# Queries spread one unit later, key weights ahead of mish, and a quarter of the first wq block brought by GpSimd's queue

## The chip, the cores and the metric

The kernel runs on one core of a Trainium2 chip. The time is device microseconds of one execution, and what is compared is the median of several runs. Everything is float32.

## The reference

A decode step for 8 batches (one token each, D = 512), as a parallel block: attention over a cache and an MLP stand beside each other and both are added to x. There are 32 query heads and 8 key heads (4 queries to a key head), 8192 cached positions and a head size of 128.

```python
xn = _layernorm(x, axis=-1)
# attention: q from xn, keys and values from the cache
q = (xn @ wq).reshape(B, 1, 32, 128).transpose(0, 2, 1, 3)
scores = einsum("bhqd,bhkd->bhqk", q, repeat(k_cache, 4)) * 128 ** -0.5
o = einsum("bhqk,bhkd->bhqd", softmax(scores), repeat(v_cache, 4))
attn = o.transpose(0, 2, 1, 3).reshape(B, 1, 32 * 128) @ wo
# MLP: Dense -> Mish -> Dense, F = 1792
h = einsum("bsd,df->bsf", xn, w1) + b1
mlp = einsum("bsf,fd->bsd", h * tanh(softplus(h)), w2)
return x + attn + mlp
```

## The kernel before

The cache is the work: keys and values are 537 MB of the 561 MB that are read. They come in units. A unit is one batch and one pair of key heads (8 query heads); there are 4 pairs times 8 batches, so 32 units, numbered j = 8 * pair + batch. Each unit has 8.39 MB of keys and 8.39 MB of values, laid by the host so that each of the 128 partitions reads one contiguous row of 64 KB (`load_unit`).

All of it goes through one wide tile `kv` of 2.5 unit rows for each partition. `V_AT` is the place of values, the first row. `K_AT` gives two places for keys that overlap by half a row: keys of even units lie in the second row, keys of odd units half a row further. So the keys of unit j+1 may be loaded as soon as the first half of the scores of unit j is through, and the values of unit j as soon as the values of unit j-1 were used. Unit 0 is an exception: its keys lie in the values' place. The weights of the MLP (`w1_t`), the bias (`b1_sb`), x and the scratch of `mish` borrow the second row at the start; the loads of wo and w2 use `kv` at the end.

Nothing is reordered by a scheduler: the order in which the code is written is the order of each engine's queue, and waits come from the data. Nearly all loads are issued by SyncE (SP), in one queue, in order: the first pair's block of wq (`load_q(0)`, 2.10 MB into tile `ws`), the keys of unit 0, w1, the keys of unit 1, and then, for unit after unit, keys j+1 and values j. ScalarE's queue issues x and b1. GpSimd issues no load; it makes `ident`, `ones`, `perm` and clears `pt8`.

The start, before the first unit: GpSimd makes the identity; VectorE builds selection matrices from it (`perm`, `mask`, `bsel` and others, lines 146 to 166) and then does the layer norm (lines 170 to 183); TensorE turns the normalised x into `xn4` (for wq) and `xnT` (for w1); `selections` fills tile `tr` with a selection matrix; `project` multiplies `xn4` with `ws` into PSUM tile H, in two halves of 512 columns (L218), and turns the result into `qT`; `spread` multiplies 16 slices of `tr` with `qT` into PSUM tile X (L244) and copies them to `qr` (L251); `key_weights(0)` multiplies `qr` with `mask` on VectorE (L262) into `wk`, the stationary operand of the scores.

One unit in the loop (lines 441 to 471), in the order of the code: half of `scores(j)` on TensorE (L279), the issue of keys j+1, the other half, `softmax(j)` (a chain of small steps, from L291 to L312), `values(j-1)` on TensorE (L341), the issue of values j, `key_weights(j+1)` on VectorE, `turn(j)` (TensorE permutes the exponentials into X at L318, VectorE transposes X into `tr` at L323 and sums into `pt8` at L329), and `merge(j-1)`. In unit 0 `mish` stands in the place of `values`, ahead of the issue of values 0 and of `key_weights(1)`.

Every pair of key heads needs its own queries. With `LOAD_Q, MAKE_Q, SPREAD_Q = 4, 5, 6` the next block of wq is loaded at the end of batch 4 of a pair, `project` runs in batch 5 ahead of `turn`, and `selections` and `spread` run at the end of batch 6, after `turn` and `merge`. `selections` overwrites `tr`, which `turn` has just used.

Of the kernel before, what the change touches and what calls it, by code (L numbers as in the profile page):

```python
# [8 lines left out]
F32 = mybir.dt.float32  # L9
# [4 lines left out]
P = 128  # L14
B = 8
# [3 lines left out]
DH = 128  # L19
# [5 lines left out]
G = 4  # L25
NH = 2
TG = SK // (NH * G) // P
BW = 1024
CC = D // P
FG = F // G  # L30
FT = 4
FP = FG // FT
Q = P // G
# [4 lines left out]
ROW = NB * P * BW // P  # L38
# [13 lines left out]

V_AT = 0
K_AT = (ROW, ROW + ROW // 2)
W1_AT = ROW
# [1 line left out]
PLACES = 2 * ROW + ROW // 2  # L59


LOAD_Q, MAKE_Q, SPREAD_Q = 4, 5, 6


@with_exitstack
def kernel(
# [12 lines left out]
    nc = tc.nc  # L79
# [7 lines left out]
    kv = const.tile([P, PLACES], F32, name="kv")  # L87
# [13 lines left out]
    hsel = const.tile([P, H2], F32, name="hsel")  # L101
    isel = const.tile([P, TL], F32, name="isel")
    rsel = const.tile([P, H2], F32, name="rsel")
    gsel = const.tile([G, G, B], F32, name="gsel")
    xn4 = const.tile([P, CC, B], F32, name="xn4")
    xnT = const.tile([P, CC, B], F32, name="xnT")
    qr = const.tile([P, DI, H2 * B], F32, name="qr")
    xres = const.tile([P, P], F32, name="xres")
    oT = const.tile([P, NP, H2, B], F32, name="oT")
# [4 lines left out]
    def load_q(m):  # L114

        rows = wq.rearrange("j p f -> (j p f)").rearrange("(m p f) -> m p f", m=NP, p=P)
        nc.sync.dma_start(ws, rows[m])

    def load_unit(src, j, at):
        m, b = divmod(j, B)  # L120
        lo = (b * HKV + 2 * m) * NH * G
        t = kv[:, at : at + ROW]
        nc.sync.dma_start(
            t,
            src[lo : lo + NB].rearrange("j p f -> (j p f)").rearrange("(p f) -> p f", p=P),
        )
        return t
# [2 lines left out]
    low = kv[:B, W1_AT : W1_AT + 3 * D]  # L130
    x_sb, xc, sq = (low[:, i * D : (i + 1) * D] for i in range(3))
    nc.scalar.dma_start(x_sb, x)
    b1_sb = kv[:G, W1_AT + 7168 : W1_AT + 7168 + FG]
    nc.scalar.dma_start(b1_sb, b1.rearrange("(g f) -> g f", g=G))
    load_q(0)
    k_t = {0: load_unit(kT, 0, V_AT)}
    w1_t = kv[:, W1_AT : W1_AT + 7168].rearrange("p (j f) -> p j f", j=2 * CC)

# [19 lines left out]
    for d in range(2):  # L158
# [3 lines left out]
            axis=AX.XY,  # L162
        )
    nc.vector.tensor_copy(
        gsel, ident[:G, :G].rearrange("p (g o) -> p g o", o=1).to_broadcast([G, G, B])
    )


# [17 lines left out]
    for c in range(CC):  # L186
        nc.tensor.transpose(
            M[:, 32 + c * B : 32 + (c + 1) * B], xc[:, c * P : (c + 1) * P], ident[:B, :B]
        )
    nc.vector.tensor_copy(xn4.rearrange("p c b -> p (c b)"), M[:, 0:32])  # L190
    nc.vector.tensor_copy(xnT.rearrange("p c b -> p (c b)"), M[:, 32:64])
    for g in range(G):
# [17 lines left out]
    selections()  # L210


    def project():

        w = ws.rearrange("p (c f) -> p c f", c=CC)
        for d in range(2):
            for c in range(CC):
                nc.tensor.matmul(  # L218
                    H[Q * c : Q * c + B, :],
                    xn4[:, c, :],  # L220
                    w[:, c, d * 512 : (d + 1) * 512],
                    start=True,
                    stop=True,
                )
            qp = work.tile([P, 512], F32, name="e")
            nc.scalar.copy(qp, H)  # L226
            for h in range(REP):
                at = 192 + (d * REP + h) * B
                nc.tensor.matmul(  # L229
                    M[:, at : at + B],  # L230
                    qp[:, h * DH : (h + 1) * DH],
                    bsel[:, :B],
                    start=True,
                    stop=True,
                )
        qT = work.tile([P, H2 * B], F32, name="qT", bufs=1)
        nc.vector.tensor_scalar_mul(qT, M[:, 192 : 192 + H2 * B], DH**-0.5)
        return qT
# [18 lines left out]
    def key_weights(j):  # L257
        b = j % B
        w = WK[j] = work.tile([P, DI, 2, NH * G, REP], F32, name="wk", bufs=1)
        q = qr.rearrange("p i (d o h b) -> p i d o h b", d=2, o=1, b=B)[..., b]  # L260
        for d in range(2):
            nc.vector.tensor_mul(  # L262
                w[:, :, d],
                q[:, :, d].to_broadcast([P, DI, NH * G, REP]),
                mask[:, d * NH * G : (d + 1) * NH * G]
                .rearrange("p (o k r) -> p o k r", o=1, r=1)
                .to_broadcast([P, DI, NH * G, REP]),
            )
# [68 lines left out]
    def values(j, vt):  # L337
        for n in range(NJ):
            l, c = divmod(n, HALF)
            q = n % G  # L340
            nc.tensor.matmul(  # L341
                O[Q * q : Q * (q + 1), :],
                pt8[:, c, TL * l : TL * (l + 1), :].rearrange("p t h -> p (t h)"),
                vt[:, 512 * n : 512 * (n + 1)],
                start=(n < G),
                stop=(n >= NJ - G),
            )
        os = work.tile([P, DH], F32, name="os")
        nc.vector.tensor_scalar(os, O[:, :DH], isel[:, 0:1], None, op0=ALU.mult)  # L349
        for i in range(1, TL):  # L350
            nc.vector.scalar_tensor_tensor(  # L351
                os, O[:, DH * i : DH * (i + 1)], isel[:, i : i + 1], os, op0=ALU.mult, op1=ALU.add
            )
        return os
# [6 lines left out]

    def mish(w1_t, b1_sb, flat):
        hp = H[:, :FG]
        for g in range(G):
            nc.tensor.matmul(
                hp[Q * g : Q * g + B, :], gsel[:, g, :], b1_sb, start=True, stop=False
            )
        for c in range(CC):
            for g in range(G):
                nc.tensor.matmul(  # L370
                    hp[Q * g : Q * g + B, :],
                    xnT[:, c, :],
                    w1_t[:, c * 2 + g // 2, g % 2 * FG : (g % 2 + 1) * FG],
                    start=False,
                    stop=(c == CC - 1),
                )
        a, z, z2, one, h = (flat[:, FG * i : FG * (i + 1)] for i in range(5))
        nc.vector.tensor_copy(h, hp)
        nc.vector.scalar_tensor_tensor(a, h, -1.0, h, op0=ALU.mult, op1=ALU.max)
        nc.scalar.activation(z, a, AF.Exp, scale=-1.0)  # L380
        nc.vector.tensor_mul(z2, z, z)
        m = a
        nc.vector.tensor_single_scalar(m, h, 0.0, op=ALU.is_gt)
        nc.vector.tensor_scalar(one, z2, -1.0, 1.0, op0=ALU.mult, op1=ALU.add)
        nc.vector.tensor_mul(one, one, m)
        t1 = m
        nc.vector.tensor_add(t1, one, z2)
        t2 = z2
        nc.vector.tensor_scalar(one, one, -1.0, 1.0, op0=ALU.mult, op1=ALU.add)
        nc.vector.scalar_tensor_tensor(t2, z, 2.0, t1, op0=ALU.mult, op1=ALU.add)  # L390
        nc.vector.scalar_tensor_tensor(t1, one, 2.0, t2, op0=ALU.mult, op1=ALU.add)
        nc.vector.reciprocal(z, t1)
        nc.vector.tensor_mul(t1, t2, z)
        act = one
        half = FG // 2
        for e in range(2):
            nc.vector.tensor_mul(
                act.rearrange("p (i a e l) -> p e a l i", a=2, e=2, i=W2R)[:, e],
                h[:, half * e : half * (e + 1)].rearrange("p (a l i) -> p a l i", a=2, i=W2R),
                t1[:, half * e : half * (e + 1)].rearrange("p (a l i) -> p a l i", a=2, i=W2R),  # L400
            )
        turned = flat[:, 5 * FG : 6 * FG]
        nc.vector.transpose(turned, act)
        nc.vector.tensor_copy(aT, turned.rearrange("p (j q) -> p j q", q=Q)[:, :, :B])
# [27 lines left out]


    nc.sync.dma_start(w1_t, w1.rearrange("j p f -> p j f"))
    k_t[1] = load_unit(kT, 1, K_AT[1])
    qT = project()
    spread(qT)
    key_weights(0)

# [1 line left out]
    for j in range(UNITS):  # L441
        b = j % B
        more = j // B + 1 < NP

        k = k_t.pop(j)
        scores(j, k, j % 2 == 1, 0)
        if j == UNITS - 1:
            v_t[j] = load_unit(v, j, K_AT[0])
        elif j > 0:
            k_t[j + 1] = load_unit(kT, j + 1, K_AT[(j + 1) % 2])  # L450
        scores(j, k, j % 2 == 0, 1)
        WK.pop(j)
        lsel = softmax(j)
        os = None
        if j > 0:
            os = values(j - 1, v_t.pop(j - 1))
        else:
            mish(w1_t, b1_sb, kv[:, W1_AT : W1_AT + 6 * FG])
        if j + 1 < UNITS:
            v_t[j] = load_unit(v, j, V_AT)  # L460
            key_weights(j + 1)
        if more and b == LOAD_Q:
            load_q(j // B + 1)
        if more and b == MAKE_Q:
            qT = project()
        turn(j, lsel)
        if j > 0:
            merge(j - 1, os)
        if more and b == SPREAD_Q:
            selections()  # L470
            spread(qT)


    w_o = [kv[:, 4096 * m : 4096 * (m + 1)] for m in range(NP)]
# [28 lines left out]
        )  # L503
    for p, t in zip(parts[1:], w2_t[1:]):
        down(*p, t)
    res = work.tile([P, DH], F32, name="os")
    nc.vector.tensor_add(res, H[:, :P], xres)
    nc.sync.dma_start(out, res)

# [37 lines left out]
```

## Time and profile before

| | |
|---|---|
| median of 3 runs | 1332.83 us (1330.54 to 1333.72) |
| the profiled execution | 1329.46 us |
| its span in the profile | 1327.7 us |
| busy | PE 75%, PEld 26%, DVE 39%, ACT 3%, POOL 0% |
| mean granted TensorE clock | 0.869 |
| read from HBM | 561.01 MB, mean 423 GB/s over the span |

Times in the views are microseconds from the start of the span. PE is TensorE's matmul, PEld its weight load, DVE is VectorE, ACT ScalarE, POOL GpSimd, SP SyncE; a "q" behind an engine is its sequencer, which issues DMAs. A float32 matmul shows as two matmul instructions, so that the 32 matmuls of `scores` stand as x64. "DMA share" in a table of windows is the mean busy share of the 16 DMA engines; it can go a little over 1. The chain that ended last is the work followed back from the last instruction, each step to what released it.

### The profile page before, as it was taken

How to read it: one execution, taken by the hardware profiler on the slowest of the kernel's cores; microseconds unless marked ns; L12 is line 12 of the kernel's file. 1: busy time of each engine (PE TensorE's matmuls, PEld its weight loads, DVE VectorE, ACT ScalarE, POOL GpSimd, SP SyncE). 2: the span in 40 equal slices, each digit the busy share in tenths (PEclk: the TensorE clock that was granted, in tenths of full speed). 3: DMA queues.
4: the chain of work that ended last, by engine and by line, in shares of the span. 5: the costliest groups of instructions: out<-in, count | busy, mean ns of one | idle time of the engine just before them, and what ended most of it. 6: DMA issues, size and time to landing. Idle time of an engine off the chain costs nothing.

```text
span 1327.7 us, 11151 instructions
## 1 busy us (share of the span) xinstructions
PE 990.3 (75%) x5040; PEld 349.4 (26%) x5040; DVE 514.8 (39%) x728; ACT 40.2 (3%) x88; POOL 2.2 (0%) x9
## 2 busy tenths in 40 slices
PE   5688767878887678785877677788686687677666
PEld 3222222323222222233322222232332222222222
DVE  3464344431444433345243344413444423344421
ACT  1000000000000000000000000000000000000000
POOL 0000000000000000000000000000000000000000
PEclk9999888787988898877998788788697988888897
DMA  9999999998999999999999999999899999999998
GB/s 394 443 407 418 439 440 418 439 435 340 431 439 441 417 433 439 435 433 427 393 433 423 435 439 431 431 429 439 370 417 435 439 437 423 432 439 437 429 414 334
DMA packets 13591, 561.79 MB, mean 423 GB/s; under 512 B 1244, under 2 KB 1376, under 8 KB 4584
## 3 DMA queue, kind: packets, MB, share of 16 engines
q1 hardware_dynamic: 13520, 561.06, 98.2%
q8 instruction: 39, 0.64, 0.2%
q14 instruction: 8, 0.07, 0.0%
q10 hardware_dynamic: 24, 0.02, 0.0%
HBM read 561.01 MB, written 0.07 MB: 423 GB/s over the span
## 4 chain that ended last, share of the span: by engine, by line
DMA 65%; PE 29%; DVE 5%; ACT 1%; issue 0%; SPq 0%
DMA kv<-in_v 62%; PE o L341 19%; PE s L279 6%; DMA kv<-in_w 3%; PE x L244 2%; DVE pt L329 2%; PE x L318 1%; DVE tr L323 1%; DVE tr L205 0%; PE h L425 0%; DVE wk L262 0%; PE m L229 0%; PE h L218 0%; DVE nm L291 0%; PE h L370 0%
## 5 line engine op out<-in xcount | busy, mean ns | idle before, releaser
L279 PE MATMUL s<-kv,wk 128*64 128x512 f32 x2048 | 507.4, 659 | 165.7 <-DMA kv<-in_kT 153.1
L341 PE MATMUL o<-kv,pt 128*32 128x512 f32 x2048 | 258.5, 663 | 51.8 <-DMA kv<-in_v 42.2
L279 PEld LDWEIGHTS s<-kv,wk 128*64 128x64 f32 x2048 | 156.3, 152 | 491.6 <-issue 322.9
L329 DVE TENSOR_REDUCE pt<-tr 64x512 f32<-64x2048 f32 x64 | 241.4, 3771 | 1.6
L291 DVE TENSOR_REDUCE nm<-s 128x1 f32<-128x512 f32 x32 | 22.1, 692 | 413.5 <-PE s L279 413.5
L318 PE MATMUL x<-e,perm 128*128 128x512 f32 x256 | 126.7, 641 | 0.0
L341 PEld LDWEIGHTS o<-kv,pt 128*32 128x32 f32 x2048 | 68.2, 120 | 215.5 <-issue 161.2
L349 DVE TENSOR_SCALAR os<-o,isel 128x128 f32<-128x128 f32 x32 | 11.2, 351 | 261.1 <-PE o L341 261.1
L323 DVE STREAM_TRANSPOSE tr<-x 128x512 f32<-128x512 f32 x128 | 78.7, 673 | 0.0
L318 PEld LDWEIGHTS x<-e,perm 128*128 128x128 f32 x256 | 49.3, 203 | 75.1 <-issue 75.1
L262 DVE TENSOR_TENSOR wk<-qr,mask 128x512 f32<-128x512 f32 x64 | 62.9, 1023 | 8.7 <-ACT qr L251 8.7
L244 PE MATMUL x<-qT,tr 128*128 128x64 f32 x128 | 29.4, 424 | 37.7 <-DVE tr L205 34.7
L310 ACT ACTIVATE e<-s,nmx 128x512 f32<-128x512 f32 x32 | 22.0, 687 | 1058.0 <-DVE nmx L307 1058.0
L244 PEld LDWEIGHTS x<-qT,tr 128*128 128x128 f32 x128 | 27.9, 330 | 38.8 <-DVE tr L205 35.0
L351 DVE SCALAR_TENSOR_TENSOR os<-o,isel,os 128x128 f32<-128x128 f32 x96 | 33.7, 351 | 3.4
L292 PE MATMUL m<-ident,nm 128*1 128x128 f32 x32 | 8.6, 270 | 25.5 <-DVE nm L291 25.5
L303 PE MATMUL m<-ident,nx 1*128 1x1 f32 x32 | 7.0, 218 | 24.1 <-DVE nx L299 24.1
L358 PE MATMUL m<-hsel,os 128*128 128x8 f32 x64 | 12.4, 266 | 9.3 <-DVE rt L321 9.3
L312 DVE TENSOR_SCALAR lsel<-rsel,l 128x8 f32<-128x8 f32 x32 | 7.4, 231 | 30.4 <-ACT e L310 30.4
L321 DVE RECIPROCAL rt<-m 128x8 f32<-128x8 f32 x32 | 6.6, 207 | 29.7 <-PE m L319 29.7
L292 PEld LDWEIGHTS m<-ident,nm 128*1 128x1 f32 x32 | 2.5, 79 | 53.7 <-DVE nm L291 53.7
L229 PE MATMUL m<-bsel,e 128*128 128x8 f32 x64 | 11.8, 313 | 6.0 <-ACT e L226 6.0
(88 smaller groups left out, 165.7 us busy)
## 6 DMA issues: line engine op xcount, KB each, us to landing
ws<-in_wq SPq DMA_DIRECT2D x4, 2048.0 KB, 34.3
kv<-in_wo SPq DMA_DIRECT2D x4, 2048.0 KB, 24.3
kv<-in_w SPq DMA_DIRECT2D x1, 3584.0 KB, 26.6
kv<-in_w SPq DMA_DIRECT2D x1, 2048.0 KB, 35.6
kv<-in_w SPq DMA_DIRECT2D x1, 1024.0 KB, 20.7
kv<-in_kT SPq DMA_DIRECT2D x32, 29.6
kv<-in_v SPq DMA_DIRECT2D x32, 30.0
kv<-in_w SPq DMA_DIRECT2D x1, 512.0 KB, 20.5
```

The costliest lines, as they stand in the source:

```text
L229: nc.tensor.matmul(M[:, at : at + B], qp[:, h * DH : (h + 1) * DH], bsel[:, :B], start=True, stop=True,)
L244: nc.tensor.matmul(X[:, half, k * 64 : (k + 1) * 64], wide[:, half * 8 + k], qT, start=True, stop=True,)
L262: nc.vector.tensor_mul(w[:, :, d], q[:, :, d].to_broadcast([P, DI, NH * G, REP]), mask[:, d * NH * G : (d + 1) * NH * G] .rearrange("p (o ...
L279: nc.tensor.matmul(S[64 * c : 64 * (c + 1), :], w[:, i].rearrange("p d k h -> p (d k h)"), kk[:, i, c, :], start=(part == 0 and n == 0), s ...
L291: nc.vector.tensor_reduce(nm, S, axis=AX.X, op=ALU.max, negate=True)
L310: nc.scalar.activation(e, S, AF.Exp, bias=nmx, accum_out=l)
L318: nc.tensor.matmul(X[:, g], perm[:, g], e, start=True, stop=True)
L323: nc.vector.transpose(tr.rearrange("p (l t) c -> p t l c", t=TL)[:, tl], X.rearrange("p g (t q l) -> p t l g q", t=TL, q=PP)[:, tl],)
L329: nc.vector.tensor_reduce(pt8[half, :, :, d * REP : (d + 1) * REP].rearrange("p c y h -> p y c h"), tr[half].rearrange("p y (g c h) -> p y ...
L341: nc.tensor.matmul(O[Q * q : Q * (q + 1), :], pt8[:, c, TL * l : TL * (l + 1), :].rearrange("p t h -> p (t h)"), vt[:, 512 * n : 512 * (n ...
L351: nc.vector.scalar_tensor_tensor(os, O[:, DH * i : DH * (i + 1)], isel[:, i : i + 1], os, op0=ALU.mult, op1=ALU.add)
L358: nc.tensor.matmul(M[:, 168 : 168 + H2], os, hsel, start=True, stop=True)
```

## The change

- `SPREAD_Q` becomes 7. `spread` runs in batch 7, after `values` and the issue of the next load and ahead of `key_weights` of the next pair's first unit, and so ahead of `turn`. `selections` stays at the end of batch 6.
- In unit 0, `mish` comes after the issue of values 0 and after `key_weights(1)`. In it the bias is added after the products with w1, and by 8 matmuls of 224 columns for 4 of 448.
- The first block of wq is split. Three quarters (rows 0 to 383, 12 KB for each of 128 partitions) go to `ws` by SP as before. The last quarter (128 rows, 0.52 MB) goes to partitions 64 to 95 of `kv`, 16 KB for each, at the place where the keys of unit 1 will lie. GpSimd's queue brings it in four DMAs of eight partitions, each after one of four small DMAs for b1. These eight DMAs stand ahead of the making of the identity on GpSimd.
- For that, x is also turned into `xn3` (3 transposes) and `xnx` (4 matmuls to partitions 64 to 95), and `project(0)` has 7 terms for each half instead of 4. The keys of unit 1 are issued after `project(0)`, since they overwrite the quarter.
- The tile `os` has one buffer for two.

```diff
+D3 = 3
+XQ = slice(64, 96)
+XAT = ROW + ROW // 2
-LOAD_Q, MAKE_Q, SPREAD_Q = 4, 5, 6
+LOAD_Q, MAKE_Q, SPREAD_Q = 4, 5, 7
...
-    gsel = const.tile([G, G, B], F32, name="gsel")
+    gsel = const.tile([B, B, B], F32, name="gsel")
+    xn3 = const.tile([P, D3, B], F32, name="xn3")
+    xnx = const.tile([P, CC, B], F32, name="xnx")
...
-    b1_sb = kv[:G, W1_AT + 7168 : W1_AT + 7168 + FG]
-    nc.scalar.dma_start(b1_sb, b1.rearrange("(g f) -> g f", g=G))
-    load_q(0)
+    b1_sb = kv[:B, W1_AT + 7168 : W1_AT + 7168 + FG // 2]
+    q0 = wq[:CC].rearrange("j p f -> (j p) f")
+    q0_3 = ws[:, : D3 * BW]
+    q0_x = kv[XQ, XAT : XAT + CC * BW]
+    for r in range(4):
+        n = FG // 8
+        nc.gpsimd.dma_start(
+            b1_sb[:, n * r : n * (r + 1)], b1.rearrange("(g c f) -> c g f", g=B, c=4)[r]
+        )
+        nc.gpsimd.dma_start(
+            q0_x[r::4], q0[D3 * P :].rearrange("(e r i) f -> r e (i f)", r=4, i=CC)[r]
+        )
+    nc.sync.dma_start(q0_3, q0[: D3 * P].rearrange("(p i) f -> p (i f)", i=D3))
     k_t = {0: load_unit(kT, 0, V_AT)}
...
+    for c in range(D3):
+        nc.tensor.transpose(
+            M[:, 64 + c * B : 64 + (c + 1) * B], xc[:, c : D3 * P : D3], ident[:B, :B]
+        )
+    for c in range(CC):
+        nc.tensor.matmul(
+            M[XQ, 96 + c * B : 96 + (c + 1) * B],
+            xc[:, D3 * P + c :: CC],
+            ident[:B, :B],
+            start=True,
+            stop=True,
+        )
+    nc.vector.tensor_copy(xn3.rearrange("p c b -> p (c b)"), M[:, 64 : 64 + D3 * B])
+    nc.vector.tensor_copy(xnx[XQ].rearrange("p c b -> p (c b)"), M[XQ, 96:128])
...
-    def project():
+    def project(m):
         w = ws.rearrange("p (c f) -> p c f", c=CC)
+        terms = [(c, xn4[:, c, :], w[:, c]) for c in range(CC)]
+        if m == 0:
+            wx = q0_x.rearrange("p (c f) -> p c f", c=CC)
+            terms = [(c, xn3[:, c, :], w[:, c]) for c in range(D3)]
+            terms += [((c + D3) % CC, xnx[XQ, c, :], wx[:, c]) for c in range(CC)]
         for d in range(2):
-            for c in range(CC):
+            for n, (c, xt, wt) in enumerate(terms):
                 nc.tensor.matmul(
                     H[Q * c : Q * c + B, :],
-                    xn4[:, c, :],
-                    w[:, c, d * 512 : (d + 1) * 512],
-                    start=True,
-                    stop=True,
+                    xt,
+                    wt[:, d * 512 : (d + 1) * 512],
+                    start=(n < CC),
+                    stop=(n >= len(terms) - CC),
                 )
...
     nc.sync.dma_start(w1_t, w1.rearrange("j p f -> p j f"))
+    qT = project(0)
     k_t[1] = load_unit(kT, 1, K_AT[1])
-    qT = project()
     spread(qT)
     key_weights(0)
...
             os = values(j - 1, v_t.pop(j - 1))
-        else:
-            mish(w1_t, b1_sb, kv[:, W1_AT : W1_AT + 6 * FG])
         if j + 1 < UNITS:
             v_t[j] = load_unit(v, j, V_AT)
+            if more and b == SPREAD_Q:
+                spread(qT)
             key_weights(j + 1)
+        if j == 0:
+            mish(w1_t, b1_sb, kv[:, W1_AT : W1_AT + 6 * FG])
         if more and b == LOAD_Q:
             load_q(j // B + 1)
         if more and b == MAKE_Q:
-            qT = project()
+            qT = project(j // B + 1)
         turn(j, lsel)
         if j > 0:
             merge(j - 1, os)
-        if more and b == SPREAD_Q:
+        if more and b == SPREAD_Q - 1:
             selections()
-            spread(qT)
```

More of the change, by code (lines that the diff above doesn't have):

```diff
@@ L164 @@
     nc.vector.tensor_copy(
-        gsel, ident[:G, :G].rearrange("p (g o) -> p g o", o=1).to_broadcast([G, G, B])
+        gsel, ident[:B, :B].rearrange("p (g o) -> p g o", o=1).to_broadcast([B, B, B])
     )
@@ L347, in values @@
             )
-        os = work.tile([P, DH], F32, name="os")
+        os = work.tile([P, DH], F32, name="os", bufs=1)
         nc.vector.tensor_scalar(os, O[:, :DH], isel[:, 0:1], None, op0=ALU.mult)
@@ L363, in mish @@
         hp = H[:, :FG]
[L364 to L367, printed above, removed]
         for c in range(CC):
@@ L373, in mish @@
                     w1_t[:, c * 2 + g // 2, g % 2 * FG : (g % 2 + 1) * FG],
+                    start=(c == 0),
+                    stop=False,
+                )
+        for g in range(G):
+            for e in range(2):
+                nc.tensor.matmul(
+                    hp[Q * g : Q * g + B, e * (FG // 2) : (e + 1) * (FG // 2)],
+                    gsel[:, 2 * g + e, :],
+                    b1_sb,
                     start=False,
-                    stop=(c == CC - 1),
+                    stop=(e == 1),
                 )
@@ L505 @@
         down(*p, t)
-    res = work.tile([P, DH], F32, name="os")
+    res = work.tile([P, DH], F32, name="os", bufs=1)
     nc.vector.tensor_add(res, H[:, :P], xres)
```

## The prediction

> **What bounds the kernel now.** I read the page first, then the windows, then the chain of waits, then the timeline around each place that stood out. On the page, the digits of the DMA engines and the first line of the chain:
>
> ```profile
> DMA  9999999998999999999999999999899999999998
> ...
> q1 hardware_dynamic: 13520, 561.06, 98.2%
> ...
> DMA 65%; PE 29%; DVE 5%; ACT 1%; issue 0%; SPq 0%
> ```
>
> One queue, SP's, brings nearly all the bytes and keeps the 16 DMA engines busy. The transfers bound the kernel; a change pays only where the stream runs dry or would run dry. Windows show where (columns: stretch, its us, busy us of each engine, granted clock, DMA share, GB/s):
>
> ```profile
> 300.00:340.00 40.00, 34.70 (x172) 15.89 (x172) 7.97 (x16) 1.95 (x4) 0.00 (x0) 0.80 0.86 365
> 620.00:660.00 40.00, 33.83 (x174) 15.98 (x174) 9.21 (x19) 1.95 (x4) 0.00 (x0) 0.83 0.91 387
> 940.00:980.00 40.00, 33.55 (x172) 15.69 (x172) 9.09 (x18) 1.95 (x4) 0.00 (x0) 0.82 0.90 381
> 344.00:604.00 260.00, 198.92 (x986) 66.06 (x986) 100.25 (x137) 6.62 (x16) 0.00 (x0) 0.88 1.00 432
> ```
>
> Between pair boundaries the share is 1.00. At the three boundaries it is 0.86, 0.91 and 0.90, which is 0.33 x 40 = 13.2 us of lost streaming. The chain around the first boundary shows why, and its later rows how long the others take:
>
> ```profile
> 278.29 8.77 PE o L341 x64
> ...
> 301.22 1.80 DVE tr L205
> ...
> 303.07 3.69 PE x L244 x16
> ...
> 311.09 16.32 PE s L279 x64
> ...
> 363.05 8.81 PE o L341 x64
> ...
> 401.74 8.54 PE o L341 x64
> ...
> 600.34 7.07 PE o L341 x64
> ...
> 681.92 8.40 PE o L341 x64
> ...
> 919.27 8.77 PE o L341 x64
> ...
> 1002.85 10.06 PE o L341 x64
> ```
>
> An undisturbed unit takes 401.74 - 363.05 = 38.7 us, 19.35 for each of its two loads. Across a boundary two units take 84.8, 81.6 and 83.6 instead of 77.4: 7.4 + 4.2 + 6.2 = 17.7 us lost. In batch 6 TensorE stands between `turn` and L244 until VectorE has finished `turn` and `selections` (L205), then spreads until 311.0, and only then starts the scores of unit 7. The next keys wait for half of these scores:
>
> ```profile
> 287.12 0.33 SPq L123 DMA_DIRECT2D kv<-in_v  x1
> ...
> 320.56 0.33 SPq L123 DMA_DIRECT2D kv<-in_kT  x1
> ```
>
> The times from issue to landing of the two load lines, L123 (keys and values) and L117 (wq), in that order:
>
> ```profile
> DMA to landing us min/median/max: 21.8/29.8/45.6
> ```
>
> ```profile
> DMA to landing us min/median/max: 7.8/34.3/34.4
> ```
>
> The minimum, 21.8, is a load issued into a dry queue: 19.35 of transfer and 2.45 of latency. So a load must be issued 2.45 us before the one ahead of it has landed. Values 6, issued at 287.12, land about 29.8 later, at 316.9; keys 8 should have been issued by 314.5 and came at 320.56.
>
> **The change: spread behind the values.** Without spread in batch 6, scores 7 start when their keys land, 316.9 - 19.35 = 297.6, are half through at 297.6 + 8.2 = 305.8 (half of L279's 16.32), and keys 8 are issued there, 8.7 us early. The same work then stands in batch 7, and I look for what is late next. Values 6 land at 316.9 and take 8.8, to 325.7; values 7 are issued there, before spread, so SP's queue loses nothing. Spread takes 303.07 to 311.0, 8.0 us, to 333.7, and no longer waits for `selections`, which VectorE made a unit earlier. Then ScalarE's copy (0.6, by the gaps in the chain) and VectorE's key weights (1.9, L262 below), to 336.3, while TensorE does `turn` (about 4) to 338. Keys 8 landed at 336.3; scores 8 start at 338, and keys 9 are issued at 346.2. They are needed by 336.3 + 19.35 - 2.45 = 353.2. Seven us of cover remain, so no new gap. If that cover were gone, spread's 8 us would return as a gap one unit later.
>
> What comes back is between the lost share, 13.2, and the lost time of the units, 17.7. The second holds delays of single DMA engines (a load lands with its slowest engine), part of which may come back at other places. I take the middle, **15.5 us**.
>
> **Key weights ahead of mish.** The rows of the start that the rest needs:
>
> ```profile
> 0.73 0.59 ACTq L132 DMA_DIRECT2D kv<-in_x  x1
> ...
> 1.35 0.26 ACTq L134 DMA_DIRECT2D kv<-in_b  x1
> ...
> 1.38 0.53 POOL L142 MEMSET perm<- 128x512 f32 x1
> ...
> 2.40 0.64 DVE L151 COPY perm<-ident 128x16 f32<-128x16 f32 x8
> ...
> 9.96 0.57 PE L187 MATMUL m<-ident,kv 8*128 8x8 f32 x4
> ...
> 10.68 0.18 DVE L191 COPY xnT<-m 128x32 f32<-128x32 f32 x1
> ...
> 11.46 1.90 PE L218 MATMUL h<-ws,xn 128*8 128x512 f32 x8
> ...
> 12.07 8.05 SPq L123 DMA_DIRECT2D kv<-in_kT  x1
> ...
> 47.63 0.33 SPq L123 DMA_DIRECT2D kv<-in_v  x1
> ...
> 49.56 0.93 PE L365 MATMUL h<-kv,gsel 4*8 4x448 f32 x8
> ...
> 53.68 0.62 DVE L378 COPY kv<-h 128x448 f32<-128x448 f32 x1 [1.44 <-PE h L370]
> ...
> 65.15 0.22 DVE L404 COPY aT<-kv 128x112 f32<-128x112 f32 x1
> ...
> 65.28 1.92 DVE L262 TENSOR_TENSOR wk<-qr,mask 128x512 f32<-128x512 f32 x2
> ...
> 75.80 0.33 SPq L123 DMA_DIRECT2D kv<-in_kT  x1
> ```
>
> Keys 1, issued at 12.07 into a full queue (the 45.6 of the landings), land at 57.7; values 0 at 57.7 + 19.35 = 77.0. Keys 2 come at 75.80, 1.25 us after the 74.55 that would have kept the stream whole. Scores 1 had waited for L262, which stood behind mish. Ahead of mish it falls mostly into VectorE's 1.44 us of idling, mish ends at about 66 (half a us later), and scores 1 start when TensorE has done `turn`, at about 58. Keys 2, which overwrite mish's scratch too, are then issued at 66. Gain **1.2 us**. The bias matmuls (0.93 for four) become eight of half the width: at most 0.9 us more, under the cover of the 8 us by which keys 2 are now early. `os` with one buffer is free: its reader `merge` ends a unit before the next write.
>
> **The start.** Values 0 must be issued by 57.7 - 2.45 = 55.2, and they came at 47.63: a start later by up to 7.6 us costs nothing, and what is beyond is lost in full (keys 2 move along, since mish and scores 1 move as much as values 0). Two clocks can make it late.
>
> First GpSimd. It now issues eight DMAs ahead of the identity, and L151, with all of VectorE's chain behind it, waits for identity and `perm`. The trace has no issue by GpSimd. The nearest rows are ScalarE's, 0.26 and 0.59; the dearest issue is SP's 8.05 into a full queue. I take 0.59: 4.7 us, of which 0.5 is covered (perm ends at 1.91, L151 starts at 2.40). The extra transposes and matmuls cost about 1.0 (seven, at 0.57 for four), two copies 0.3, and six more terms in `project` 6 x 1.90 / 4 = 2.85. Sum 4.2 + 1.0 + 0.3 + 2.85 = 8.3, so 0.7 lost. The Trainium skill, "DMA: Bandwidth & Descriptors", section Latency and other measured facts, gives about 1 us to the first byte of GpSimd's path; eight of those would be an estimated 4.0 lost instead of 0.7, which no row here can show; the sum would stay, since the second clock is later.
>
> Second, the quarter itself. `project(0)` needs all four pieces. Its transfer shares the engines with keys 0, whose rows are 64 KB, eight on each engine, 19.35 / 8 = 2.4 us each. Lower bound: all wq landed at 0.74 + 7.8 = 8.5 before. Upper: keys 0 land at 8.5 + 19.35 = 27.9, and after that only short w1 rows compete. I take alternation with these rows: three quarters of wq are through at 8.5 x 0.75 = 6.4, the first piece goes with them, and three more pieces, data and completion, take six turns of 2.4, so it lands near 6.4 + 14.5 + 1 = 22. From the first product to the issue of values 0 it was 47.63 - 11.46 = 36.2; behind the landing stand the last four terms of the first half, as before, and seven in the second, 1.4 more. Values 0 are issued at 22 + 37.6 = 59.6, or **4.4 us lost**; the bounds are 0 and 27.9 + 37.6 - 55.2 = 10.3. This clock is the later one. The keys of unit 1 move on SP's queue past `project(0)`, to about 30; w1 ends near 57.7 - 19.35 = 38, so they are in time, and values 0, behind them on SP, wait longer anyway.
>
> **Sum.** 15.5 + 1.2 - 4.4 = 12.3 us off. The profiled execution took 1329.46 (span 1327.7 and 1.8 around it), so 1317.2; the median of the runs stands 3.4 above that execution, which gives 1320.5.
>
> **The rivals.**
> - The quarter waits out keys 0. Nothing shows that a piece gets a turn after each 64 KB row; if a queue holds the engine for all eight, the last piece lands at 27.9 and 10.3 are lost: 1332.8 - 16.7 + 10.3 = 1326.4. The skill's same page, section Queues, rings and completion order, says that an engine drains a packet of typically 9 to 17 descriptors before it goes to the next queue, which would be this case; the trace of before has no two long transfers in different queues to test it.
> - Slower: GpSimd's issues are dear. At x us each, values 0 are late by 8x - 4.0 beyond the cover. The 16.7 gained are used up at x = 2.6, and the kernel is slower by over 0.3% from 3.1. At 4 us it would be 28 - 16.7 = 11 over: 1344. For it: all of VectorE's start hangs on this queue. Against: the rows of 0.26 and 0.59.
> - Spread makes the gap again one unit later (7.0 us of cover gone, for instance because `turn` in batch 7 waits for more than I see). Then the boundaries gain nothing: 1332.8 - 1.2 + 4.4 = 1336.
> - The quarter is never waited for (it lands by 17.6): 1316.
>
> **How the numbers follow.** A measurement of this kernel can tell about 0.3%, 4 us, from no change. Forecast 0.55 and the early quarter 0.1 (both faster), the waiting quarter 0.17 (faster, 6 us), dear issues 0.07 (slower mostly), the returned gap 0.05 (within or slower), the rest, something at the start that I don't see, 0.06. Faster 0.82, within 0.3% 0.09, slower 0.09. Range: low end 17.7 + 1.2 and nothing lost, 1314, and 1 us for the reading of the lost units; high end 13.2 + 1.2 and 10.3 lost, 1328.7, and 1 us.
>
> **What would show it.** Right: DMA share near 1.00 in the windows of the three boundaries, L244 in batch 7 after L341 without a long wait for L205, keys 8, 16 and 24 issued about 9 us ahead of the landing before them, and keys 2 ahead of the landing of values 0. The start shows the two clocks: the start of L151, the wait of L218 at its fourth term, and the issue of values 0 against 55.2. Wrong: a dip that stays at a boundary or comes one unit later, L218 waiting beyond 30, or L151 beyond 15.

## The result and the profile after

The changed kernel takes 1333.2 us (median of 12 runs, 1331.34 to 1334.99); beside it the kernel before took 1331.45 (12 runs). The ratio is 1.001, 95% interval 0.9999 to 1.0021: no change, where 12 us less were forecast. The profiled execution has a span of 1330.5 us (1327.7 before).

The page after, the digits of the DMA engines and what they moved in each of the 40 slices of 33 us:

```profile
DMA  9889999999999999999999999999999999999997
GB/s 341 338 346 432 420 438 436 436 428 436 428 436 434 434 432 428 427 439 438 426 432 432 438 430 434 426 438 434 430 430 434 432 434 436 428 428 434 430 415 321
```

From the fourth slice on it is one even stream, without the three dips of before. The first three slices have become poor. Windows, columns as in the prediction:

```profile
8.00:32.00 24.00, 4.37 (x33) 2.09 (x33) 6.40 (x22) 2.21 (x4) 0.00 (x0) 1.00 0.95 349
60.00:76.00 16.00, 14.45 (x74) 4.50 (x74) 1.48 (x6) 1.12 (x1) 0.00 (x0) 1.00 0.35 131
300.00:340.00 40.00, 27.87 (x134) 9.01 (x130) 17.09 (x22) 0.78 (x2) 0.00 (x0) 0.83 1.00 433
620.00:660.00 40.00, 28.40 (x142) 9.14 (x141) 16.96 (x22) 0.78 (x2) 0.00 (x0) 0.87 0.99 430
940.00:980.00 40.00, 29.32 (x170) 11.89 (x169) 16.32 (x22) 1.95 (x4) 0.00 (x0) 0.91 1.02 440
```

The boundaries have the shares 1.00, 0.99 and 1.02 where they had 0.86, 0.91 and 0.90. Between 60 and 76 the stream is dry: share 0.35. The timeline of the start says why (line numbers are those of the changed kernel: L147 are b1's small DMAs, L150 the quarter's, L169 was L151, L255 was L218, L131 was L123):

```profile
1.26 0.65 POOL L147 DMA_DIRECT2D kv<-in_b  x1 [0.82 <-POOLq L577]
1.91 0.52 POOL L150 DMA_DIRECT2D kv<-in_wq  x1
...
4.97 0.52 POOL L150 DMA_DIRECT2D kv<-in_wq  x1
...
6.72 0.99 DVE L169 COPY perm<-ident 128x16 f32<-128x16 f32 x8 [4.23 <-POOL perm L160]
...
17.45 1.89 PE L255 MATMUL h<-ws,xn 128*8 128x512 f32 x6
...
34.05 1.89 PE L255 MATMUL h<-kv,xnx 32*8 32x512 f32 x8 [14.71 <-DMA kv<-in_wq]
...
42.20 0.34 SPq L131 DMA_DIRECT2D kv<-in_kT  x1
...
72.60 0.33 SPq L131 DMA_DIRECT2D kv<-in_v  x1
...
90.79 0.33 SPq L131 DMA_DIRECT2D kv<-in_kT  x1
```

TensorE begins `project(0)` at 17.45, does three terms, and waits 14.7 us for the quarter, until 34.05. Keys 1, behind `project(0)`, are issued at 42.20 instead of 12.07, and values 0 at 72.60 instead of 47.63. The time from issue to landing of the eight DMAs, one by one in the order of their issue, and then of keys 0 (the last figure of each line, in us):

```profile
kv<-in_b POOLq DMA_DIRECT2D x1, 1.8 KB, 6.2
kv<-in_wq POOLq DMA_DIRECT2D x1, 128.0 KB, 10.9
kv<-in_b POOLq DMA_DIRECT2D x1, 1.8 KB, 15.8
kv<-in_wq POOLq DMA_DIRECT2D x1, 128.0 KB, 21.6
kv<-in_b POOLq DMA_DIRECT2D x1, 1.8 KB, 26.5
kv<-in_wq POOLq DMA_DIRECT2D x1, 128.0 KB, 28.7
kv<-in_b POOLq DMA_DIRECT2D x1, 1.8 KB, 28.4
kv<-in_wq POOLq DMA_DIRECT2D x1, 128.0 KB, 28.9
```

```profile
kv<-in_kT SPq DMA_DIRECT2D x1, 31.2
```

With the times of issue, the first five have landed at 7.5, 12.8, 18.2, 24.5 and 30.0: 5.4 to 6.3 us apart, the 1.8 KB of b1 like the 128 KB of the quarter. Keys 0, issued at 1.19, land at 32.4 (27.9 before), and the last three come right behind them, at 32.6, 32.9 and 33.9.

One number splits every run in two: the landing of values 1, which the chain shows as the end of its first transfer. Before:

```profile
91.73 26.49 DMA kv<-in_v
```

After:

```profile
111.55 23.89 DMA kv<-in_v
```

Values 1 land at 118.2 before and at 135.4 after: 17.2 us lost by then. From there to the end of the span it is 1327.7 - 118.2 = 1209.5 before and 1330.5 - 135.4 = 1195.1 after: 14.4 us gained. The change does what it is said to do at the boundaries, and the start takes it back.

### The profile page after: what moved, and what is told of

It reads as the page before. It is cut to its first block, busy times and chain, and to the rows that moved or that the text cites. A ratio compares the mean times of both kernels' runs of the same rounds, so it can differ in the third digit from the quotient of the medians.

```text
span 1330.5 us, 11234 instructions
## 1 busy us (share of the span) xinstructions
PE 984.8 (74%) x5071; PEld 338.3 (25%) x5071; DVE 516.0 (39%) x730; ACT 40.2 (3%) x88; POOL 6.4 (0%) x17
## 4 chain that ended last, share of the span: by engine, by line
DMA 73%; PE 22%; DVE 2%; SPq 2%; issue 0%; POOL 0%; ACT 0%; DVEq 0%; POOLq 0%
DMA kv<-in_v 70%; PE o L378 19%; DMA kv<-in_wq 2%; DMA kv<-in_w 2%; SPq L528 2%; PE s L316 1%; DVE pt L366 1%; PE x L281 1%; PE h L255 0%; PE m L266 0%; PE h L403 0%; DVE kv L434 0%; DVE tr L360 0%; POOL kv L147 0%; DVE wk L299 0%
## 5 line engine op out<-in xcount | busy, mean ns | idle before, releaser
L378 PE MATMUL o<-kv,pt 128*32 128x512 f32 x2048 | 262.3, 671 | 51.8 <-DMA kv<-in_v 42.2
L328 DVE TENSOR_REDUCE nm<-s 128x1 f32<-128x512 f32 x32 | 22.1, 692 | 374.2 <-PE s L316 374.1
L281 PE MATMUL x<-qT,tr 128*128 128x64 f32 x128 | 19.3, 315 | 3.0 <-ACT qr L288 2.7
L281 PEld LDWEIGHTS x<-qT,tr 128*128 128x128 f32 x128 | 18.1, 226 | 6.2 <-ACT qr L288 3.3
L356 PEld LDWEIGHTS m<-lsel,ones 128*128 128x128 f32 x64 | 12.2, 190 | 15.6 <-issue 15.3
```

The source lines that it names most:

```text
L281: nc.tensor.matmul(X[:, half, k * 64 : (k + 1) * 64], wide[:, half * 8 + k], qT, start=True, stop=True,)
L328: nc.vector.tensor_reduce(nm, S, axis=AX.X, op=ALU.max, negate=True)
L378: nc.tensor.matmul(O[Q * q : Q * (q + 1), :], pt8[:, c, TL * l : TL * (l + 1), :].rearrange("p t h -> p (t h)"), vt[:, 512 * n : 512 * (n ...
```

## The experiments

Theory A: the boundaries gain some 15 us, and the quarter eats them, because every small DMA on a second queue has to take its turns behind the 64 KB rows of keys 0. The trace of the changed kernel has every packet with its time, and shows such turns: a row of keys 0 ends at 14.65, a 224 B packet of b1 follows at once, the next row runs from 14.66 to 17.63, a 4 B packet follows (taken to be a completion), and the row after that starts at 17.63. The trace does not name the engine of a packet; these are put together by their times. A DMA's data and its completion thus cost two rows, about the 5.4 us above. In the table, "start" is the landing of values 1 and "rest" the span less that, both from the profiled execution. Each ratio is to runs of the kernel before on the same chip.

| kernel | median us | ratio (95%) | start | rest |
|---|---|---|---|---|
| before | 1331.45 | | 118.2 | 1209.5 |
| changed | 1333.2 | 1.001 (0.9999 to 1.0021) | 135.4 | 1195.1 |
| no quarter | 1312.54 | 0.9856 (0.9832 to 0.9881) | 115.5 | 1195.1 |
| quarter only | 1354.92 | 1.0174 (1.0148 to 1.0200) | 142.1 | 1210.8 |
| spread only | 1318.41 | 0.9896 (0.9866 to 0.9926) | 121.5 | 1196.4 |
| one GpSimd DMA | 1314.62 | 0.9874 (0.9848 to 0.9899) | 117.6 | 1195.0 |
| four GpSimd DMAs, b1 on ScalarE | 1323.74 | 0.9946 (0.9930 to 0.9962) | 126.2 | 1196.0 |
| eight DMAs on ScalarE | 1331.85 | 1.0005 (0.9990 to 1.0020) | 133.6 | 1195.7 |
| keys 0 in short rows | 1319.98 | 0.9916 (0.9890 to 0.9942) | 120.5 | 1197.4 |
| quarter on SP | 1314.27 | 0.9874 (0.9846 to 0.9903) | 116.5 | 1195.6 |
| identity first | 1331.18 | 0.9996 (0.9984 to 1.0008) | 135.2 | 1195.4 |

**The two halves apart.** First the kernel before with the two moves and nothing of the quarter:

```diff
-LOAD_Q, MAKE_Q, SPREAD_Q = 4, 5, 6
+LOAD_Q, MAKE_Q, SPREAD_Q = 4, 5, 7
...
             v_t[j] = load_unit(v, j, V_AT)
+            if more and b == SPREAD_Q:
+                spread(qT)
             key_weights(j + 1)
+        if j == 0:
+            mish(w1_t, b1_sb, kv[:, W1_AT : W1_AT + 6 * FG])
...
-        if more and b == SPREAD_Q:
+        if more and b == SPREAD_Q - 1:
             selections()
-            spread(qT)
```

> The kernel before with spread moved behind the values and mish moved behind the key weights, wq and b1 as before. Theory A (the quarter's late landing alone ate the gain): the dips at the three pair boundaries go, values 0 are issued near 47.6, and about 15 to 17 us come off, ratio near 0.988. Rival B (the gain at the boundaries is given back because one slow DMA engine falls further behind when no dip lets it catch up): at most 8 us come off, ratio above 0.994.

Then the changed kernel with these lines put back, so that the quarter alone is left:

> The changed kernel with spread and mish put back to their old places: only the quarter of wq and b1 by GpSimd's queue are new. Theory A: the queue runs dry ahead of values 0 as in the changed kernel, the boundary dips stay, 16 to 18 us slower, ratio near 1.013. Rival C (the start costs little, the boundaries gained little): within 5 us of before.

The moves alone take off 18.8 us (1312.54 against 1331.37), the quarter alone adds 23.6 (1354.92). The first transfers of their chains, no quarter and then quarter only:

```profile
87.89 27.61 DMA kv<-in_v
```

```profile
115.62 26.43 DMA kv<-in_v
```

The rest is 1195.1 without the quarter and 1210.8 without the moves, so the moves are worth 14 to 16 us after the start, with or without the quarter. Rival B, that a gain at the boundaries is given back, falls, and so does C. The quarter alone costs more than the 16 to 18 expected, since in that kernel the scores of unit 1 again stand behind mish, in a start that is late already: values 0, issued at 70.11, land at 93.3, but keys 2 are issued only at 99.69, 29.6 us after values 0 (18.2 in the changed kernel).

**Spread alone.** The same without the two `mish` lines:

> The kernel before with spread moved alone; mish, wq and b1 as before. Theory A: 14 to 16 us come off, and the kernel with mish moved too stands 1 to 2 us below this one, since keys 2 are then issued ahead of the landing of values 0. Rival D (moving mish is worth nothing, since another wait takes its place): both the same within 0.5 us.

13.0 us come off; the kernel with mish moved as well stands 5.9 below it, so rival D falls, but it isn't the 1 to 2 expected either. The rest is the same within 1.3, so the difference is at the start: values 1 land at 121.5 against 115.5. Keys 2 in the kernel with spread alone, and then in the one with mish moved:

```profile
79.00 0.33 SPq L123 DMA_DIRECT2D kv<-in_kT  x1
```

```profile
65.77 0.33 SPq L123 DMA_DIRECT2D kv<-in_kT  x1
```

Here keys 2 came 3.2 us later than the 75.80 of before, although nothing ahead of them was changed. In this profile TensorE's granted clock was lower there, in the stretch from 48 to 80:

```profile
48.00:80.00 32.00, 20.55 (x92) 6.33 (x92) 24.22 (x32) 2.64 (x4) 0.00 (x0) 0.79 0.85 365
```

It was 0.84 in the same stretch before and 0.95 with mish moved. TensorE's steps ahead of keys 2 were longer than before: the products of mish took 4.60 us and not 3.19, the first half of the scores of unit 1 9.7 and not 8.6. With mish ahead, unit 1's first scores are on the path and pay for a low clock; with mish behind, keys 2 have 8 us of cover. What the move is worth therefore depends on the clock: 2.7 us against the profile of before, 6.0 against this one.

**One DMA for eight.** The quarter in one DMA of 32 partitions on GpSimd's queue, b1 in one on ScalarE's:

```diff
-    for r in range(4):
-        n = FG // 8
-        nc.gpsimd.dma_start(b1_sb[:, n * r : n * (r + 1)], ...)
-        nc.gpsimd.dma_start(q0_x[r::4], ...)
+    nc.scalar.dma_start(b1_sb, b1.rearrange("(g f) -> g f", g=B))
+    nc.gpsimd.dma_start(q0_x, q0[D3 * P :].rearrange("(e i) f -> e (i f)", i=CC))
```

> The changed kernel with the quarter in one GpSimd DMA of 32 partitions and b1 in one DMA on ScalarE's queue. Theory A (each DMA on GpSimd's queue takes its turns behind 64 KB rows of keys 0, some 5.5 us for a DMA whatever its size): one DMA lands by about 12, the product with it does not wait, values 0 are issued near 52, and 14 to 17 us come off, ratio near 0.989. Rival E (what costs is the number of bytes beside keys 0): it lands as late as the four did, near 34, and the time stays at that of the changed kernel.

The same bytes by the same queue, but 16.8 us less than before, within 2.1 of the kernel without any quarter. The landing of the one DMA, issued at 1.23:

```profile
DMA to landing us min/median/max: 9.1/9.1/9.1
```

It has landed at 10.3, the product does not wait for it, and values 0 are issued at 53.40, inside the 55.2. Bytes are not the cost; rival E falls. What one DMA costs in the midst of long rows is not shown here: this one went beside the 12 KB rows of wq, whose three quarters landed at 10.5, ahead of nearly all of keys 0.

**Four DMAs, b1 elsewhere.** The four pieces stay as they are, b1 goes to ScalarE's queue in one DMA:

> The changed kernel with b1 in one DMA on ScalarE's queue; the quarter still in four GpSimd DMAs of eight partitions. Theory A (every DMA of the queue takes about 5.5 us beside 64 KB rows, the small ones for b1 as well): four DMAs instead of eight, the last lands near 23, values 0 are issued near 61, about 6 us are lost at the start instead of 18.7, ratio near 0.993. Rival F (the DMAs for b1 cost nothing since they carry 7 KB): the landing stays near 34, and the time that of the changed kernel.

7.3 us come off instead of nothing. The last piece, issued at 2.9, waits 22.1 us:

```profile
DMA to landing us min/median/max: 7.2/13.0/22.1
```

So it lands at 25.0, nine us sooner than with b1's four DMAs between, which carry 7 KB together. Here a DMA costs turns, not bytes; rival F falls.

**Another queue.** The eight DMAs as in the changed kernel, `nc.gpsimd` replaced by `nc.scalar`:

> The changed kernel with the same eight DMAs issued by ScalarE's queue instead of GpSimd's. Theory A (taking turns with the 64 KB rows of keys 0 costs, whichever queue it is): the last piece lands between 25 and 36, and the time is within 6 us of the changed kernel. Rival G (GpSimd's path itself is slow, some 5 us for each DMA): they land by 15, and 14 to 17 us come off.

No change from the changed kernel (1331.85 against 1333.2). From its timeline:

```profile
33.18 1.89 PE L255 MATMUL h<-kv,xnx 32*8 32x512 f32 x8 [14.06 <-DMA kv<-in_wq]
```

The product resumes at 33.18 after a wait of 14.06; with GpSimd it was 34.05 and 14.71. It is not GpSimd's path that is slow; rival G falls.

**Short rows beside it.** Only the competitor is changed: keys 0 come by four DMAs with 16 KB rows instead of one with 64 KB rows, so the length of the rows and the number of DMAs change together.

```diff
-    k_t = {0: load_unit(kT, 0, V_AT)}
+    k0 = kT[:NB].rearrange("j p f -> (j p f)").rearrange("(p f) -> p f", p=P)
+    for i in range(4):
+        at = slice(i * ROW // 4, (i + 1) * ROW // 4)
+        nc.sync.dma_start(kv[:, V_AT + at.start : V_AT + at.stop], k0[:, at])
+    k_t = {0: kv[:, V_AT : V_AT + ROW]}
```

> The changed kernel with keys 0 loaded by four DMAs whose rows are 16 KB instead of by one with rows of 64 KB; the same bytes, and the eight GpSimd DMAs as they are. Theory A (a turn lasts as long as one row of the other queue): a turn falls from 2.4 to 0.6 us, the last piece lands by about 15, the product does not wait for it beyond GpSimd's issues, values 0 are issued near 56, 13 to 16 us come off, ratio near 0.989. Rival G (GpSimd's path itself is slow): the landing stays near 34 and the time that of the changed kernel.

11.1 us come off. The quarter's four pieces, and the product that needs them:

```profile
DMA to landing us min/median/max: 7.3/11.1/14.9
```

```profile
20.02 1.89 PE L259 MATMUL h<-kv,xnx 32*8 32x512 f32 x8 [0.71 <-DMA kv<-in_wq]
```

The last piece lands at 19.9 instead of 33.9, and the wait falls from 14.7 to 0.7 us, with GpSimd's eight DMAs untouched. That is the direct test of the turns. The size was a little optimistic (15 was expected): the eight land 1.8 us apart in the mean, a third and not a quarter of the 5.4 to 6.3 between the first five of the changed kernel. A turn is not a whole DMA of the other queue either, since the four of keys 0 land 5 to 6 us apart. Values 0 are issued at 57.96, 2.8 after the 55.2, but values 1 land 5.0 later than without the quarter (120.5 against 115.5): keys 0, by the last of their four DMAs, land at 32.0 and not at 27.7, so the whole stream is later.

**Two more runs on the start.** The quarter in one DMA on SP's own queue, ahead of everything, and, separately, the changed kernel with GpSimd's identity made ahead of its eight DMAs:

> The changed kernel with the quarter in one DMA of 32 partitions on SP's own queue, ahead of the three quarters and keys 0, and b1 in one DMA on ScalarE's queue: no second queue beside keys 0. Theory A (sharing with a second queue delays the quarter, and the 32 partitions cost a little streaming): the quarter lands by 5, keys 0 land near 29 or earlier, the time is within 3 us of the kernel with one GpSimd DMA (1314.6). Rival H (the streaming lost while the quarter comes in, keys 0 2 us late with one GpSimd DMA, is due to two queues sharing the engines): keys 0 land at 27.9 as before, and about 2 us less than with one GpSimd DMA.

> The changed kernel with GpSimd's identity, ones, perm and pt8 made ahead of its eight DMAs instead of behind them. Theory A (the quarter's landing is the later of the two clocks at the start, so GpSimd's eight issues ahead of the identity are hidden): L151's counterpart starts near 2.5 instead of 6.7, the product still waits for the quarter until 34 to 36, and the time stays within 3 us of the changed kernel. Rival I (the late identity holds up the start): 4 us come off.

With SP the time is that of one GpSimd DMA (1314.27 against 1314.62), so a single transfer on a second queue costs nothing that the time shows; rival H falls. Both stand some 2 us above the kernel without the quarter. The extra terms of `project(0)` are not the reason, since values 0 are issued at 53.40 and 52.54, inside the 55.2. Keys 0 land later already, at 29.7 (GpSimd) and 28.8 (SP) against 27.7, and values 1 are later by about as much (117.6 and 116.5 against 115.5). So it is lost while the split block comes in; why, was not tried. With the identity first VectorE starts at 2.40 instead of 6.72, and nothing comes of it:

```profile
32.53 1.89 PE L255 MATMUL h<-kv,xnx 32*8 32x512 f32 x8 [17.87 <-DMA kv<-in_wq]
```

TensorE arrives 4.7 us earlier and waits 3.2 longer. The quarter was the later clock, as the prediction had it; rival I falls.

## Why the prediction was wrong

- **Right: the boundaries.** 15.5 us were taken, 14.4 is the gain in the rest of the changed kernel and 12 to 14.5 in the others that have the moves. Keys 8 were to come 8.7 us ahead of need; they are issued at 325.60, and values 6 land at 335.3, which is 7.3 ahead of need with the 2.45 of latency. Spread (L281) follows the values without a wait:

```profile
325.60 0.33 SPq L131 DMA_DIRECT2D kv<-in_kT  x1
...
335.39 8.37 PE L378 MATMUL o<-kv,pt 128*32 128x512 f32 x64 [0.92 <-DMA kv<-in_v]
...
343.69 2.00 PE L281 MATMUL x<-qT,tr 128*128 128x64 f32 x16
```

The gap did not return a unit later: the next use of values comes 38.7 us after this one.
- **Right: GpSimd's issues.** Taken at 0.59 each, they take 0.52; L169 starts at 6.72, 4.3 later (4.2 forecast), and is hidden behind the quarter, as the identity-first kernel shows.
- **Right in the mechanism, at the start:** 7.6 us free and the remainder lost in full. Values 0 were issued at 72.60, 17.4 after 55.2, and values 1 landed 17.2 later than before. Against the kernel with the same moves and no quarter they landed 19.9 later (135.4 against 115.5), so some 2.5 were lost beyond the sum: values 0, issued dry, took 23.1 us to land where 21.8 was taken, and the rest is open. Keys 1 were taken to be in time and were not: w1 landed at 42.3, and they were issued only at 42.20. That cost nothing more, since they landed at 65.4, before values 0 were issued.
- **Wrong: the landing of the quarter.** This is the step that failed: 22 was taken, with bounds of 8.5 and 27.9; it was 33.9, outside them. L255 waited until 34.05, the prediction's own sign of being wrong (beyond 30). Two things were left out. The count of turns held only the quarter's DMAs, though b1's four stand between them on the same queue: with those gone it landed at 25.0, near the 22. Only five of the eight had landed when keys 0 did. And the upper bound took keys 0's landing of before, while keys 0 themselves stream slower beside the small DMAs (349 GB/s from 8 to 32, 400 in the same stretch before; they landed at 32.4, not 27.9) and the last pieces come only behind them. With 33.9 in the prediction's own sum, 33.9 + 37.6 - 55.2 = 16.3 us are lost, against 16.7 gained: no change, as measured. That the two are so nearly equal is a coincidence.
- **The rivals.** "The quarter waits out keys 0" was nearest in its place and too low in its price, for the bound just named. The rule that it cited (the Trainium skill, "DMA: Bandwidth & Descriptors", Queues, rings and completion order: an engine drains a packet of typically 9 to 17 descriptors before it goes to the next queue) does not fit beside keys 0: DMAs landed between keys 0's eight rows on an engine, 5.4 to 6.3 us apart, the packets at 14.65 and 17.63 each follow one row, and the spacing shrank with the row when that was cut. The measurement decides for turns of one row, two for a DMA.
- **Key weights ahead of mish** was sized 1.2 from the profile of before. Against that profile keys 2 land 1.5 us earlier (96.1 against 97.6) and values 1 2.7; why the one grows into the other is open. Against spread alone it was 6.0, since TensorE's clock in that stretch was lower there; the prediction took it as fixed.

## What to carry to other kernels

A small DMA beside a stream of long rows is not priced by its bytes: here it cost about two rows of the other queue, each time, so a transfer that something waits for goes in one piece, or ahead on the same queue, or beside short rows. Count every DMA on a queue, the trivial ones too. When a change has several parts, measure them apart: here the moves alone are worth 1.4% (0.9856), and the version without the quarter beats both kernels.

## What the runs showed of the hardware that was not expected

DMA share hides this loss: from 8 to 32 the engines are 0.95 busy after and 0.94 before, at 349 and 400 GB/s. A busy share near 1 is no full stream.

An even stream is still not quite steady. In the chain of the changed kernel the uses of values are 38.70 us apart, but now and then 40.26:

```profile
806.21 8.53 PE o L378 x64
...
844.91 7.12 PE o L378 x64
...
885.17 7.12 PE o L378 x64
```

There are four such steps of 1.5 us, 272 to 277 us apart, without a dip. In the landings of the trace, one DMA engine falls 1.5 us further behind the others at each; the page has 39 instruction loads of 16 KB, one in some 34 us, and each step comes with the first load to land after every eighth of them (those at 304.3, 581.6, 849.3 and 1124.2). That this is the cause is argued, not shown.
